# First batch of a fused attention and two-MLP kernel: another order of the weight conversions, other buffers, later scores

## Chip, cores, metric

One NeuronCore of a Trainium2 chip runs the whole program. The metric is device microseconds (us) of one execution. The kernel before takes a median of 846.8 us over three runs (846.05 to 849.2).

## What is computed

```python
scores = x @ state.T / sqrt(64)            # per batch (8) and head (8): 512 tokens, 32 state rows
xread  = softmax(scores) @ state           # 512 rows
sread  = softmax(scores.T) @ x             # 32 rows
x1 = concat(xread, sread)                  # 8 batches x 544 tokens x 512
h  = relu(x1 @ w_in)                       # 1024 features, padded at both ends
c  = conv_w[0]*h[t-1] + conv_w[1]*h[t] + conv_w[2]*h[t+1]
y  = (h * sigmoid(c)) @ w_out
k  = relu(mix_k(y) @ w_k);  r = sigmoid(mix_r(y) @ w_r);  out = r * (k*k @ w_v)
```

The weights come as 64-bit floats. The kernel reads their bits as pairs of 32-bit words and makes 32-bit values out of them on ScalarE (ACT) and VectorE (DVE).

## The kernel before

The work runs in slots. A slot is one token tile `t` (tiles 0 to 7 are the 512 tokens of a batch, tile 8 the state rows) and one block `f` of 128 features (8 of them). `g1_main` makes the product `hps` of the slot, `g1_a` drains it to `hb` (with relu) and starts the convolution, `g1_b` makes the gate `g`, `g1_c` splits it into a high and a low part `gs`, and `g1_sec` adds the slot's share of `y` to `acc` with three products for each of four output blocks: one with the high part (line 132), one each at lines 133 and 134 that need the low part as well or follow it. Batch 0 takes plain 32-bit products; for its first three blocks the convolution runs on TensorE (PE) too (`cps`, line 487), for all others on ACT (line 491) and DVE (line 493).

`x1 @ w_in` is never formed from `x1`: per batch, `m` (line 298) multiplies `state` with `w_in` into `p_m`, which is drained to `m_first` (batch 0) or `m_odd`/`me` (others), and `hps` is the softmax of the scores times that. The softmax of a batch (`max1`, `exp1`, `norm1`, `turn1`) is worked on DVE and ACT from the scores `p_s` (line 317) and ends in `a_first` (batch 0, line 374) or `aring` (others, lines 379 and 380). `exp2`, `turn2`, `sread` and `sturn` make the state rows.

At the start everything is missing. `w_in` and `w_out` come as four units each (two feature blocks, two transfers of 512 KB) and every unit is converted by `split` (lines 178 to 189): two passes on ACT (178 Abs, 180 Copy) and three on DVE (181, 182, 184), 1024 columns wide, and for `w_out` one more on ACT (188) and DVE (189). The first half of unit 0 of `w_in` is converted alone, 512 columns wide. PE is given idle products of the identity (`warm`, line 1079), 12 before the first scores, 14 behind them and 12 behind the first `m`.

A scheduler turns this into one instruction order per engine, by a priority for each piece. `at_half(k, fn, prio)` files a piece under half slot `k` (two per slot); `behind(i)` keeps what is written under it out of the order until `i` stands there; it adds no wait at run time. `attend(b, k, first)` files the attention of batch `b` from half slot `k` on, `M_PARTS` says at which half slots before the batch its products `m` come, and `weight_at` files load and conversion of a weight unit. Each engine then runs its list strictly in order. All transfers are issued by SP from one queue, with up to eight in flight: the ninth waits until the first has landed.

Of the kernel before, what the change touches and what calls it, by code (L numbers as in the profile page):

```python
# [25 lines left out]
ATTEND = 3  # L26
# [5 lines left out]
WARM = (12, 14, 12)  # L32
ATTEND_0, ATTEND_1 = 9, 3
# [3 lines left out]
def tile_kernel(  # L37
# [99 lines left out]
    class Weights:  # L137
# [24 lines left out]
        def split(self, w, first=0, whole=False):  # L162
# [21 lines left out]
            last = nc.vector.scalar_tensor_tensor(to, x, 3, v, op0=ALU.logical_shift_left, op1=ALU.bitwise_or)  # L184
# [25 lines left out]
    def weight(src, key, tag, pool, k, many, group):  # L210


        r = Weights([src[k + i] for i in range(many)], many, N, stg)

        def split(first=0, n=many):
            g = (key, "group", k // group)
            if k % group == 0 and first == 0:
                W[g] = pool.tile([P, 2, group, N], F32R, tag=f"{tag}{k // group}", name=f"{key}{k}")
            o = k % group + first
            for i in range(n):  # L220
                W[key, k + first + i] = W[g][:, :, o + i]
            return r.split(W[g][:, :, o:o + n], first)

        return r.load, split
# [57 lines left out]
    class Attention:  # L282
# [54 lines left out]
        def max1(self, g):  # L337
            q = self.q[:, g]
            nc.vector.transpose(q, self.v["s", g])
            q3 = q.rearrange("p (a n) -> p a n", n=NS)  # L340
            m1 = self.s1[:, g, 0]
            nc.vector.tensor_reduce(m1, q3, axis=AX.X, op=ALU.max)
            self.sub = nc.vector.tensor_tensor(
                q3, q3, m1.unsqueeze(2).to_broadcast([P, M1, NS]), op=ALU.subtract
            )
# [85 lines left out]
    anchors, y_stored, gated, last_ks = {}, {}, {}, {}  # L431
# [14 lines left out]
    def g1_main(t, f):  # L446
        p = ps_h.tile([P, 512], F32, tag="h", name="hps")
        if t < B:
            if t == 0:
                sl = slice(f * P, f * P + P)  # L450
                for g in range(G):
                    nc.tensor.matmul(p, m_first[:, g, sl], a_first[:, g], start=g == 0, stop=g == G - 1)
                st1[t, f] = {"p": p}
                return
# [42 lines left out]
    def g1_b(t, f):  # L497
# [5 lines left out]
        nc.vector.scalar_tensor_tensor(  # L503
# [557 lines left out]
    win = [weight_in(2 * i, 2, early[:, i] if i < 2 else None) for i in range(KF // 2)]  # L1061
# [32 lines left out]
    win[0][1](0, 1)  # L1094
# [3 lines left out]
    for g in range(G):  # L1098
        a.max1(g)
# [4 lines left out]
    for g in range(G):  # L1104
        a.turn1(g)
    with behind(a.sub):
        second = win[0][1](1, 1)
    second_m = a.m(1, 1)
    diagonals(0)
    nc.vector.tensor_scalar(om, muc, scalar1=-1.0, scalar2=1.0, op0=ALU.mult, op1=ALU.add)  # L1110
    with behind(second), behind(first_m):
        wout[0][1]()
    with behind(second):
        for g in range(G):
            a.max2(g)
    a.neg2()
    with behind(second_m):
        for g in range(G):
            a.exp2(g)

    def attend(b, k, first):
# [3 lines left out]
        if not first:  # L1125
# [9 lines left out]
            for i, d in enumerate(M_PARTS):  # L1135
                at_half(h + d, lambda i=i: a_.m(4 * i, 4), prio=500 * (h + d) - M_AHEAD)
# [23 lines left out]
    for f in range(1, KF):  # L1160
        if f % 2 == 0:
            weight_at(win[f // 2], 2 * f - 1, max(0, 2 * f - 5))
            at_half(2 * f - 1, lambda f=f: a.m(f, 2))
        if f < CONV_ON_PE:
            at_half(2 * f - 1, lambda f=f: diagonals(f))
    for f in range(2, KF, 2):
        weight_at(wout[f // 2], 2 * f + 5, 2 * f + 2)
    at_half(0, lambda: load_s(1, ap), lambda: load_t(1, ap), prio=-500)
    at_half(0, lambda: load_n(0, ap), prio=0)
    attend(0, ATTEND_0, True)  # L1170
    for b in range(1, B):
        attend(b, (b - 1) * H1 + (ATTEND if b > 1 else ATTEND_1), False)
    early_k = {j: weight_early(w_k, "k", 2 * j, h) for j, h in EARLY_AT.items()}
    for k, h in EARLY_V.items():
        load, split = weight(w_v, "v", "wa", wp, k, 2, 4)
# [130 lines left out]
```

## Time and profile before

| | |
|---|---|
| median of 3 runs | 846.8 us |
| the profiled execution itself | 847.35 us |
| its span, first to last instruction | 845.6 us |
| PE busy | 823.9 us, 97% |
| DVE busy | 694.9 us, 82% |
| ACT busy | 617.6 us, 73% |
| share of PE in the chain that ended last | 90% |
| mean granted TensorE clock | 0.992 of 2.4 GHz |

The table is an average over stages. The profile's 40 slices of the span show PE at 9 tenths or more everywhere but in the first, the third and the last slice (7, 8 and 7 tenths), and the granted clock below 9 tenths in the second slice alone. So the opening stretch, some 80 us long, has to be read by itself, wait by wait, in the order of time.

### The profile page before, as it was taken

Reading aid. Unit: us, or ns where it says so; the run is one execution under the profiler, and the core shown is the slowest. Engines: PE = TensorE matmul, PEld = TensorE weight load, DVE = VectorE, ACT = ScalarE, POOL = GpSimd, SP = SyncE. Lnnn points to the kernel's source line nnn. Section 1 sums busy time; section 2 is a strip of 40 time slices with the busy share of each in tenths; the row PEclk is TensorE's granted clock in tenths of the full one; section 3 lists DMA queues with packets and bytes.
Section 4 is the critical chain, followed back from the end, with each engine's and each line's share of the span. In section 5 each row is a group of like instructions: output and inputs, shape, how many; then the busy total and the mean of one; then the engine's idle time right before and its main releaser. Section 6 shows DMA issues by size and latency. Waiting matters only on the chain.

```text
span 845.6 us, 15213 instructions
## 1 busy us (share of the span) xinstructions
PE 823.9 (97%) x5766; PEld 701.8 (83%) x5766; DVE 694.9 (82%) x1110; ACT 617.6 (73%) x1163; POOL 10.3 (1%) x99
## 2 busy tenths in 40 slices
PE   7989999999999999999999999999999999999997
PEld 5345776676777666789998889999999999999997
DVE  5898787989988989887999789696978869596673
ACT  5688748678868688988976679767776876776652
POOL 0000000000000000000000000000000000000000
PEclk9899999999999999999999999999999999999999
DMA  9344312240505330905524855777878677775675
GB/s 340 131 147 156 107 50 107 78 179 7 199 30 179 129 112 1 349 26 193 199 84 175 282 190 174 226 239 247 255 228 262 217 239 260 227 251 180 218 253 194
DMA packets 68873, 150.50 MB, mean 178 GB/s; under 512 B 16064, under 2 KB 39616, under 8 KB 65984
## 3 DMA queue, kind: packets, MB, share of 16 engines
q1 hardware_dynamic: 68800, 149.53, 52.5%
q8 instruction: 45, 0.74, 0.4%
q14 instruction: 28, 0.23, 0.1%
HBM read 118.55 MB, written 30.97 MB: 177 GB/s over the span
## 4 chain that ended last, share of the span: by engine, by line
PE 90%; DVE 4%; ACT 3%; DMA 2%; issue 1%; SPq 0%; ACTq 0%; DVEq 0%
PE acc L132 14%; PE acc L133 13%; PE acc L134 13%; PE vps L133 6%; PE vps L132 6%; PE vps L134 6%; PE rps L133 3%; PE rps L134 3%; PE rps L132 3%; PE hps L132 3%; PE hps L134 3%; PE hps L133 3%; PE p_m L298 2%; PE hps L463 2%; PE p_s L317 2%; PE kps L132 1%
## 5 line engine op out<-in xcount | busy, mean ns | idle before, releaser
L493 DVE SCALAR_TENSOR_TENSOR cacc<-hb,vcol,cacc 128x512 f32<-128x512 f32 (+1 forms) x138 | 97.4, 719 | 19.7 <-ACT cacc L491 18.7
L133 PE MATMUL acc<-gs,out 128*128 128x512 f32 (+1 forms) x288 | 111.0, 386 | 0.2 <-DVE gs L512 0.2
L134 PE MATMUL acc<-gs,out 128*128 128x512 f32 (+1 forms) x288 | 109.7, 381 | 0.0
L132 PE MATMUL acc<-gs,out 128*128 128x512 f32 (+1 forms) x288 | 93.4, 396 | 1.2 <-ACT gs L511 0.6
L132 PEld LDWEIGHTS acc<-gs,out 128*128 128x128 f32 x288 | 53.0, 189 | 23.5 <-issue 4.2
L133 PEld LDWEIGHTS acc<-gs,out 128*128 128x128 f32 x288 | 54.2, 188 | 15.9 <-DVE aT L377 1.7
L134 PEld LDWEIGHTS acc<-gs,out 128*128 128x128 f32 x288 | 54.2, 188 | 12.6 <-issue 2.8
L132 PE MATMUL acc<-xo,k 128*128 128x256 f32 x224 | 63.3, 282 | 0.9 <-ACT stage L686 0.9
L134 PE MATMUL acc<-xo,k 128*128 128x256 f32 x224 | 63.1, 282 | 0.0
L133 PE MATMUL acc<-xo,k 128*128 128x256 f32 x224 | 62.9, 281 | 0.0
L511 ACT ACTIVATE gs<-g 128x512 fp32r<-128x512 f32 (+1 forms) x72 | 44.1, 612 | 17.9 <-PE acc L134 10.2
L512 DVE TENSOR_TENSOR gs<-g,gs 128x512 fp32r<-128x512 f32 (+1 forms) x72 | 47.0, 659 | 4.7 <-ACT gs L511 4.5
L503 DVE SCALAR_TENSOR_TENSOR g<-g,hb 128x512 f32<-128x512 f32 (+1 forms) x72 | 47.2, 657 | 3.4 <-ACT g L502 3.0
L475 ACT ACTIVATE hb<-hps 128x512 f32<-128x512 f32 x64 | 38.0, 599 | 16.4 <-PE hps L134 9.6
L132 PE MATMUL acc<-xo,kT 128*128 128x256 f32 x168 | 48.4, 288 | 1.0 <-ACT acc L855 1.0
L133 PE MATMUL acc<-xo,kT 128*128 128x256 f32 x168 | 48.4, 288 | 0.8 <-DVE xo L687 0.8
L491 ACT ACTIVATE cacc<-hb,vcol 128x512 f32<-128x512 f32 (+1 forms) x69 | 48.3, 701 | 0.4
L134 PE MATMUL acc<-xo,kT 128*128 128x256 f32 x168 | 48.3, 287 | 0.0
L133 PE MATMUL vps<-va,xa 128*128 128x256 f32 x168 | 47.6, 283 | 0.0
L132 PE MATMUL vps<-va,xa 128*128 128x256 f32 x168 | 47.6, 283 | 0.0
L134 PE MATMUL vps<-va,xa 128*128 128x256 f32 x168 | 47.5, 283 | 0.0
L502 ACT ACTIVATE g<-cacc 128x512 f32<-128x512 f32 (+1 forms) x69 | 42.2, 612 | 7.0 <-DVE cacc L493 6.2
(265 smaller groups left out, 2615.4 us busy)
## 6 DMA issues: line engine op xcount, KB each, us to landing
va<-vdT SPq DMA_DIRECT2D x38, 512.0 KB, 4.4
va<-vdB SPq DMA_DIRECT2D x28, 512.0 KB, 4.5
vb<-vdT SPq DMA_DIRECT2D x18, 512.0 KB, 4.2
xT<-x_t SPq DMA_DIRECT2D x32, 256.0 KB, 3.7
xn<-x_n SPq DMA_DIRECT2D x8, 1024.0 KB, 5.8
y<-yo SPq DMA_DIRECT2D x8, 1024.0 KB, 4.1
vb<-vdB SPq DMA_DIRECT2D x14, 512.0 KB, 4.8
va<-rdT SPq DMA_DIRECT2D x14, 512.0 KB, 4.6
```

The lines of the kernel that those rows point to most:

```text
L132: nc.tensor.matmul(ps, lh, rh, start=start and k == 0, stop=False, **how)
L133: nc.tensor.matmul(ps, lh, rl, start=False, stop=False, **how)
L134: nc.tensor.matmul(ps, ll, rh, start=False, stop=stop and k == last, **how)
L298: self.m_mm = nc.tensor.matmul(p[g][cols, :n * P].rearrange("p (f c) -> p f c", c=P), sT[self.b][r, c, h % 2], win_f[r, f:f + n, c * P:(c ...
L317: last = nc.tensor.matmul(self.v["s", g][cols, :], sT[self.b][r, h // 2, h % 2], xT[self.b][r, h // 2], start=True, stop=True,)
L475: nc.scalar.activation(hb[:, 1:1 + S], s["p"], AF.Relu)
L491: nc.scalar.activation(a[:, :n], hb[:, 0:n], AF.Copy, scale=w[0])
L493: nc.vector.scalar_tensor_tensor(a[:, :n], hb[:, k:k + n], w[k], a[:, :n], op0=ALU.mult, op1=ALU.add)
L502: nc.scalar.activation(g[:, :n], s["a"][:, :n], AF.Tanh, scale=0.5)
L503: nc.vector.scalar_tensor_tensor(g[:, :n], g[:, :n], 1.0, s["hb"][:, 1:1 + n], op0=ALU.add, op1=ALU.mult)
L511: act = nc.scalar.activation(gs[:, 0, :n], s["g"][:, :n], AF.Copy)
L512: dve = nc.vector.tensor_tensor(gs[:, 1, :n], s["g"][:, :n], gs[:, 0, :n].bitcast(F32), op=ALU.subtract)
```

## The change

It moves work within the opening and changes nothing that is computed.

- The idle products become 9 before the scores, 14 behind them, 12 behind the first `m`, and 6 new ones between the two halves of the first `hps` product.
- The first softmax is filed before the first conversion of `w_in`. The second half of unit 0 now stands behind unit 0 of `w_out`.
- Units 1 to 3 of `w_in` and `w_out` are filed by the tables `FIRST_IN` (half slot of the conversion, gate, half slot of `m`, half slot of the load) and `FIRST_OUT` (half slot of the conversion, gate, half slot of the load). The conversion stands behind the gate instruction `g` of the named slot.
- Units 2 and 3 of `w_in` are loaded into `early2`, a new tile in the place that `w_v` uses later (tag `wa1`), instead of the staging tile `raw`.
- The rest of batch 0's attention starts at half slot 5 instead of 9, batch 1's scores at 8 instead of 3, and batch 1's two `m` at half slots 14 and 15 instead of 10 and 12. Two loads move from half slot 0 to 1 and 4.

```diff
-WARM = (12, 14, 12)
-ATTEND_0, ATTEND_1 = 9, 3
+WARM = (9, 14, 12, 6)
+ATTEND_0, ATTEND_AT, M_AT = 5, {1: 8}, {1: (-2, -1)}
+
+FIRST_IN = {1: (2, -1, 3, 0), 2: (5, 0, 7, 0), 3: (8, 1, 9, 2)}
+FIRST_OUT = {1: (4, 0, 1), 2: (7, 1, 4), 3: (11, 2, 8)}
...
                 for g in range(G):
-                    nc.tensor.matmul(p, m_first[:, g, sl], a_first[:, g], start=g == 0, stop=g == G - 1)
+                    first = nc.tensor.matmul(p, m_first[:, g, sl], a_first[:, g], start=g == 0, stop=g == G - 1)
+                    if f == 0 and g == 0:
+                        with behind(first):
+                            warm(WARM[3])
...
-    win = [weight_in(2 * i, 2, early[:, i] if i < 2 else None) for i in range(KF // 2)]
+    early2 = wp.tile([P, 2, 2 * N * 2], U32, tag="wa1", name="early")
+    win = [weight_in(2 * i, 2, (early, early2)[i // 2][:, i % 2]) for i in range(KF // 2)]
...
-    win[0][1](0, 1)
+    for g in range(G):
+        a.max1(g)
+    with behind(a.turned):
+        win[0][1](0, 1)
     first_m = a.m(0, 1)
     with behind(a.m_mm):
         warm(WARM[2])
-    for g in range(G):
-        a.max1(g)
...
+    diagonals(0)
+    nc.vector.tensor_scalar(om, muc, scalar1=-1.0, scalar2=1.0, op0=ALU.mult, op1=ALU.add)
+    with behind(a.sub), behind(first_m):
+        wout[0][1]()
+    with behind(wout[0][2].merged):
+        for g in range(G):
+            a.max2(g)
+    a.neg2()
     with behind(a.sub):
         second = win[0][1](1, 1)
     second_m = a.m(1, 1)
...
+    for j in range(1, KF // 2):
+        w, g, m, load = FIRST_IN[j]
+        at_half(load, win[j][0])
+        at_half(w, behind_gate(win[j], g), prio=500 * w)
+        at_half(m, lambda j=j: a.m(2 * j, 2))
+        w, g, load = FIRST_OUT[j]
+        at_half(load, wout[j][0])
+        at_half(w, behind_gate(wout[j], g), prio=500 * w)
...
-    at_half(0, lambda: load_s(1, ap), lambda: load_t(1, ap), prio=-500)
-    at_half(0, lambda: load_n(0, ap), prio=0)
+    at_half(1, lambda: load_s(1, ap), lambda: load_t(1, ap), prio=-500)
+    at_half(4, lambda: load_n(0, ap), prio=0)
     attend(0, ATTEND_0, True)
     for b in range(1, B):
-        attend(b, (b - 1) * H1 + (ATTEND if b > 1 else ATTEND_1), False)
+        attend(b, ATTEND_AT.get(b, (b - 1) * H1 + ATTEND), False)
```

DVE, from the end of the small conversion of the convolution weights on: the kernel before (`early` and `mid` belong to the conversion of `w_in`, `q` to the softmax, `om` is the small mixing constant of a much later stage).

```order
L182 TENSOR_SCALAR mid<-mid 128x512
L339 STREAM_TRANSPOSE q<-p_s 128x512
L181 SCALAR_TENSOR_TENSOR early<-early 128x512
L1110 TENSOR_SCALAR om<-muc 128x8
L342 TENSOR_REDUCE s_154<-q 128x16
L339 STREAM_TRANSPOSE q<-p_s 128x512
L184 SCALAR_TENSOR_TENSOR w_in<-mid,early 128x512
```

The same place on DVE in the changed kernel.

```order
L344 STREAM_TRANSPOSE q<-p_s 128x512
L347 TENSOR_REDUCE s_152<-q 128x16
L1117 TENSOR_SCALAR om<-muc 128x8
L348 TENSOR_TENSOR q<-q,s_152 128x512
L344 STREAM_TRANSPOSE q<-p_s 128x512
L184 SCALAR_TENSOR_TENSOR early<-early 128x512
L185 TENSOR_SCALAR mid<-mid 128x512
L347 TENSOR_REDUCE s_152<-q 128x16
L372 TENSOR_REDUCE s_152<-q 128x16
L187 SCALAR_TENSOR_TENSOR w_in<-mid,early 128x512
```

The softmax's first transpose no longer stands behind a conversion pass; `om` now stands third, ahead of the second transpose, and the finished first half block of `w_in` comes three rows later.

ACT, around the first drain `hb` of batch 0: the kernel before.

```order
L178 ACTIVATE mid<-raw 128x1024
L180 ACTIVATE raw<-raw 128x1024
L355 ACTIVATE q<-q 128x512
L180 ACTIVATE early<-early 128x1024
L475 ACTIVATE hb<-hps 128x512
L476 ACTIVATE carry<-hb 128x2
L180 ACTIVATE raw<-raw 128x1024
L178 ACTIVATE mid<-early 128x1024
L502 ACTIVATE g<-cps 128x512
```

The same place on ACT in the changed kernel.

```order
L181 ACTIVATE mid<-raw 128x1024
L183 ACTIVATE raw<-raw 128x1024
L181 ACTIVATE mid<-early 128x512
L183 ACTIVATE early<-early 128x1024 x2
L183 ACTIVATE raw<-raw 128x1024
L483 ACTIVATE hb<-hps 128x512
L193 ACTIVATE out_231<-raw 128x1024
L181 ACTIVATE mid<-early 128x1024
L484 ACTIVATE carry<-hb 128x2
L181 ACTIVATE mid<-raw 128x1024
L183 ACTIVATE early<-early 128x1024
L510 ACTIVATE g<-cps 128x512
```

Ahead of `hb` there are now three full passes where there was one (the last of them, `raw`, is unit 1 of `w_out`), and four between `hb` and the gate's `g` where there were two.

PE, around batch 1's scores `p_s`: the kernel before (out_251 is unit 0 of `w_out`, out_415 unit 1).

```order
L317 MATMUL p_s<-xT,sT 32x512 x4
L452 MATMUL hps<-a_first,m_first 128x512
L317 MATMUL p_s<-xT,sT 32x512 x4
L452 MATMUL hps<-a_first,m_first 128x512
L132 MATMUL acc_376<-gs,out_251 128x512
```

The place of these scores on PE in the changed kernel (out_356 is unit 1 of `w_out`).

```order
L135 MATMUL acc_373<-gs,out_356 128x512
L423 MATMUL p_srT<-ident,sr 128x128
L322 MATMUL p_s<-xT,sT 32x512
L423 MATMUL p_srT<-ident,sr 128x128
L322 MATMUL p_s<-xT,sT 32x512 x3
L136 MATMUL acc_370<-gs,out_356 128x512
```

They stood before slot 1's share of `acc` (unit 0 of `w_out`) and now stand within slot 2's, behind the products of slots 3, 4 and 5 and the whole of batch 0's `sread`.

## Rows read from the trace of the kernel before

**Rows 1.** Stretch, length; PE, PEld, DVE, ACT, POOL busy (count); clock, DMA share, GB/s.
```profile
20.00:30.00 10.00, 8.67 (x28) 3.06 (x28) 10.00 (x15) 4.73 (x8) 0.10 (x1) 0.68 0.27 105
...
50.00:60.00 10.00, 7.89 (x37) 4.37 (x37) 9.50 (x20) 8.86 (x16) 0.48 (x1) 0.83 0.56 210
...
75.00:150.00 75.00, 75.00 (x489) 52.91 (x487) 57.57 (x95) 54.50 (x121) 1.72 (x17) 1.00 0.24 88
```

**Rows 2.** PE in order of time: start, us, what, [idle before <-its releaser].
```profile
1.41 5.11 PE L1079 MATMUL idle<-ident 128*128 128x128 f32 x24 [1.41 <-POOL hb L474]
6.45 1.54 PE L317 MATMUL p_s<-xT,sT 64*32 64x512 f32 x16
...
13.05 0.45 PE L298 MATMUL p_m<-w_in,sT 64*32 64x128 f32 x16 [1.74 <-DVE w_in L184]
13.43 2.94 PE L1079 MATMUL idle<-ident 128*128 128x128 f32 x24
17.63 1.10 PE L452 MATMUL hps<-a_first,m_first 128*128 128x512 f32 x2 [1.25 <-DVE a_first L374]
20.16 2.04 PE L452 MATMUL hps<-a_first,m_first 128*128 128x512 f32 x2 [1.44 <-DVE a_first L374]
22.90 4.59 PE L487 MATMUL cps<-hb,diag 128*128 128x512 f32 x6 [0.69 <-ACT hb L475]
...
28.35 1.98 PE L452 MATMUL hps<-a_first,m_first 128*128 128x512 f32 x4 [0.48 <-ACT m_first L305]
31.08 2.84 PE L487 MATMUL cps<-hb,diag 128*128 128x512 f32 x6 [0.75 <-ACT hb L475]
33.85 0.66 PE L298 MATMUL p_m<-w_in,sT 64*32 64x256 f32 x16
```

**Rows 3.** PE in order of time, the later part of the opening.
```profile
51.49 1.30 PE L298 MATMUL p_m<-w_in,sT 64*32 64x256 f32 x16 [2.76 <-ACT e L349]
53.38 1.77 PE L132 MATMUL acc<-gs,out 128*128 128x512 f32 x4 [0.58 <-ACT gs L511]
...
55.80 2.57 PE L452 MATMUL hps<-a_first,m_first 128*128 128x512 f32 x4
...
62.30 1.09 PE L298 MATMUL p_m<-w_in,sT 64*32 64x512 f32 x16
63.32 1.19 PE L132 MATMUL acc<-gs,out 128*128 128x512 f32 x4
...
68.33 1.23 PE L298 MATMUL p_m<-w_in,sT 64*32 64x256 f32 x16 [2.00 <-DVE m_odd L309]
...
78.20 1.06 PE L298 MATMUL p_m<-w_in,sT 64*32 64x512 f32 x8
...
79.28 0.48 PE L132 MATMUL hps<-aring,m_odd 128*128 128x512 f32 x1
```

**Rows 4.** DVE in order of time, same columns.
```profile
9.84 0.71 DVE L339 STREAM_TRANSPOSE q<-p_s 128x512 f32<-128x512 f32 x1
...
19.30 0.71 DVE L374 STREAM_TRANSPOSE a_first<-q 128x512 f32<-128x512 f32 x1
...
38.66 0.72 DVE L339 STREAM_TRANSPOSE q<-p_s 128x512 f32<-128x512 f32 x1 [0.72 <-PE p_s L317]
...
70.59 0.68 DVE L380 TENSOR_TENSOR aring<-aT,aring 128x512 fp32r<-128x512 f32 x1
```

**Rows 5.** Transfers issued from 4 to 13 us: count, KB each, us from issue to landing.
```profile
raw<-w_in SPq DMA_DIRECT2D x2, 512.0 KB, 10.8
...
muc<-mu SPq DMA_DIRECT2D x1, 4.0 KB, 5.7
```

**Rows 6.** SP's queue in order of time: start, us, what.
```profile
4.49 0.43 SPq L1069 DMA_DIRECT2D muc<-mu  x1
```

**Rows 7.** ACT in order of time: batch 0's first drain and gate.
```profile
22.24 0.60 ACT L475 ACTIVATE hb<-hps 128x512 f32<-128x512 f32 x1 [1.37 <-PE hps L452]
...
27.53 0.60 ACT L502 ACTIVATE g<-cps 128x512 f32<-128x512 f32 x1 [2.33 <-PE cps L487]
```

More of the change, by code (lines that the diff above doesn't have):

```diff
@@ L183, in split @@
             to = w.bitcast(U32) if whole else v
-            last = nc.vector.scalar_tensor_tensor(to, x, 3, v, op0=ALU.logical_shift_left, op1=ALU.bitwise_or)
+            last = self.merged = nc.vector.scalar_tensor_tensor(
+                to, x, 3, v, op0=ALU.logical_shift_left, op1=ALU.bitwise_or
+            )
             if whole:
@@ L222, in split @@
             return r.split(W[g][:, :, o:o + n], first)
-        return r.load, split
+        return r.load, split, r
     def weight_early(src, key, k, at):
@@ L338, in max1 @@
             q = self.q[:, g]
-            nc.vector.transpose(q, self.v["s", g])
+            self.turned = nc.vector.transpose(q, self.v["s", g])
             q3 = q.rearrange("p (a n) -> p a n", n=NS)
@@ L430, in tile_kernel @@
     st1 = {}
-    anchors, y_stored, gated, last_ks = {}, {}, {}, {}
+    anchors, gates, y_stored, gated, last_ks = {}, {}, {}, {}, {}
     def acc_tiles(key):
@@ L502, in g1_b @@
         nc.scalar.activation(g[:, :n], s["a"][:, :n], AF.Tanh, scale=0.5)
-        nc.vector.scalar_tensor_tensor(
+        gates[t * KF + f] = nc.vector.scalar_tensor_tensor(
             g[:, :n], g[:, :n], 1.0, s["hb"][:, 1:1 + n], op0=ALU.add, op1=ALU.mult
@@ L1108, in tile_kernel @@
     second_m = a.m(1, 1)
[L1109 to L1119, printed above, removed]
+    for g in range(G):
+        a.exp2(g)
     def attend(b, k, first):
@@ L1134, in attend @@
                 at_half(k + 3, lambda: load_s(b + 1, ap))
-            for i, d in enumerate(M_PARTS):
+            for i, d in enumerate(M_AT.get(b, M_PARTS)):
                 at_half(h + d, lambda i=i: a_.m(4 * i, 4), prio=500 * (h + d) - M_AHEAD)
@@ L1159, in tile_kernel, with behind_gate, split @@
     h2 = 2 * i0
[L1160 to L1167, printed above, removed]
-    at_half(0, lambda: load_s(1, ap), lambda: load_t(1, ap), prio=-500)
-    at_half(0, lambda: load_n(0, ap), prio=0)
+    def behind_gate(w, n):
+        def split():
+            with behind(gates[n] if n >= 0 else second):
+                w[1]()
+        return split
+    for j in range(1, KF // 2):
[6 more added lines that the diff above has]
+        at_half(w, behind_gate(wout[j], g), prio=500 * w)
+    for f in range(1, CONV_ON_PE):
+        at_half(2 * f - 1, lambda f=f: diagonals(f))
+    at_half(1, lambda: load_s(1, ap), lambda: load_t(1, ap), prio=-500)
+    at_half(4, lambda: load_n(0, ap), prio=0)
     attend(0, ATTEND_0, True)
     for b in range(1, B):
-        attend(b, (b - 1) * H1 + (ATTEND if b > 1 else ATTEND_1), False)
+        attend(b, ATTEND_AT.get(b, (b - 1) * H1 + ATTEND), False)
     early_k = {j: weight_early(w_k, "k", 2 * j, h) for j, h in EARLY_AT.items()}
     for k, h in EARLY_V.items():
-        load, split = weight(w_v, "v", "wa", wp, k, 2, 4)
+        load, split, _ = weight(w_v, "v", "wa", wp, k, 2, 4)
         at_half(h - 4, load)
```

## The prediction

> **What bounds the kernel now.** I read the busy shares first, then stretches of them, then PE by itself in the order of time, and only then the engines that PE waits for. Over the span PE is busy 97%, and from 75 to 150 us it works without a break at the full clock while DVE has 17.4 and ACT 20.5 of 75 us free [rows 1]. Nothing on DVE or ACT can be won there; whatever the change gains must be a wait or a low clock of PE in the opening. There the reader sees two kinds of loss. PE stands still: 1.74 us before the first `m`, 1.25 and 1.44 around the first `hps`, .69, .48 and .75 for the first drains [rows 2], later 2.76 (batch 1's `m`, behind the exponentials on ACT), .58 and 2.00 [rows 3]. And PE is slow: the mean granted clock is .68 from 20 to 30 us and .83 from 50 to 60 [rows 1]. Of its two levels, 1.2 and 2.4 GHz, the lower was granted for (1 − .68) × 2 × 10 = 6.4 us and (1 − .83) × 2 × 10 = 3.4 us. Each follows a stretch with two waits close together.
>
> **The change, part by part.** *The first softmax.* `p_s` is done at 6.45 + 1.54 = 7.99 us [rows 2], but the first transpose starts at 9.84 [rows 4], behind a conversion pass. The change frees it. The gain is mostly taken back by `om`, which now stands third on DVE: its `muc` is issued at 4.49 [rows 6] and lands 5.7 us later [rows 5], at 10.2, so the second transpose and the conversion passes behind it begin there, not at 8.6. With some .65 us for each 128x512 instruction (the rows of that size have .68 to .72 [rows 4] and overlap a little), the first half block of `w_in` is ready at 14.3 us instead of 13.0, and PE waits 3.1 us before the first `m` instead of 1.74. The second half of `a_first` comes at 19.1 instead of 19.30 + .71 = 20.0 [rows 4]; at full clock its half of `hps` (1.10 / 2 [rows 2]) ends at about 19.8, with pipeline and the first half 20.6 at the latest.
>
> *The first drain.* `hb` starts at 22.24 now [rows 7]. It will stand behind a pass on unit 1 of `w_out`. Transfers issued in this crowd of 512 KB took 10.8 us [rows 5]; counted in SP's order, this unit lands between 20.4 and 22.5. I take 21, and 1.1 us for the pass: `hb` at 22.1. So the early softmax is worth nothing here, what comes sooner on PE waits for ACT. Four passes follow, and the gate that came at 27.53 [rows 7] comes at 27.1; block 1's `hps` starts at 28.1 instead of 28.35 [rows 2]. **Gain .25.**
>
> *Idle products.* 38 become 41, each two entries of the trace, .213 us apiece in the first row (5.11 / 24, the low clock) and .12 behind the first `m` (2.94 / 24, full clock) [rows 2]. The three taken away stand ahead of the scores, which wait for their data. The six new ones, 6 × 2 × .12 = 1.4 us, fill the 1.44-us gap between the halves of `hps` [rows 2]. They are covered as long as `hb` waits for ACT until 22.1, 1.5 us after `hps` ends: cost nothing, and up to 1.4 if that cover goes.
>
> *Between 28 and 50 us.* The wait of .75 before block 1's `cps` [rows 2] is filled by block 0's first four `acc`. New waits: .23 (these `acc`, for the gate's `gs`) and .78 (the second half of an `hps`, for a drain of `m_first` on ACT), both from walking the new order with the durations of the rows. **Cost 1.0.**
>
> *Batch 1's scores and `m`.* PE waits at 51.49 and 53.38 because batch 1's exponentials and the gates meet 512 KB conversions on ACT, which is busy 8.86 of 10 us there, DVE 9.50 [rows 1]. With the scores at about 53 and 56 us and `m` behind them at half slots 14 and 15, the first `m` is reached at 65.55 and its exponentials are done at 65.65: the waits of 2.76, .58 and 2.00 go [rows 3], **5.34**, and .15 comes back. There is no margin at that point. Inside the `p_m` groups, 1.30 and 1.23 us against .66 for an undisturbed one of the same shape [rows 2, 3], another .64 + .57 = **1.2** of waiting goes. `m` is issued in four halves of 1.06 instead of partly whole at 1.09 [rows 3]: **cost 1.0**.
>
> *The low clock.* The second stretch follows the 2.76 and .58 us waits. Without them I expect it to go: `acc` x4 took 1.77 there and 1.19 elsewhere, `hps` x4 2.57 and 1.98 [rows 2, 3], 1.17 in these two groups, and over the 3.4 low us half of the time is lost, **1.7**. The first stretch I leave as it is, since ACT sets the end there; its rows say what it would give if it went and ACT were early: hps 2.04 − 1.10, cps 4.59 − 2.84 [rows 2], together 2.7. The page "TensorE: Matmul & The Clock Gate" of the Trainium skill, section "Terms", prices the throttled time at one minus the granted ratio, here half; for both stretches that would be 3.2 + 1.7, and the sum 3.2 us lower than mine. The rows agree on the second stretch; on the first, `hps` and `cps` account for 2.7.
>
> *Loads.* Two units of `w_in` go to `w_v`'s later place; `w_v` is loaded from half slot 42 on, and tile 1 begins at 16. They no longer wait for `raw` to come free, and the queue is not full after 30 us (DMA share .27 from 20 to 30 us [rows 1]). Counted at nothing; late landings of `w_out` unit 1 cost up to 1.5.
>
> *Sum:* idle .75 + 5.34, early .25, inside waits 1.2, clock 1.7, together 9.2; new waits 1.0 + .15, halves 1.0, together 2.2. Gain 7.0. The profiled execution took 847.35, so **840.3 us**. The median shown is .55 below it; by the same gain it would be 839.8. As a cross-check, tile 1's first `hps`, at 79.28 now [rows 3], falls to 74.35 in the walk, 4.9 earlier, and with eight `acc` products (at most 2 × 1.19) and half an `m` (1.06) more done by then [rows 3]: 7 to 8 us.
>
> **Rivals.** *DVE's debt.* At tile 1's start DVE will have nine 128x512 instructions fewer behind it (gates, `gs`, convolution sums, one `m_odd`), at .68 each [rows 4] 6.1 us. If PE meets it there, the gain is all but paid back: 846.4. For it: tile 1 leans on DVE from its first drain. Against it: DVE has 17.4 us free up to 150 [rows 1]. Chance .14.
>
> *The clock falls earlier.* If PE loses its clock in the 3.1 us before the first `m`, the 18 idle products behind it take .09 more per entry, 36 × .09 = 3.3, and `hps` .94 more: it ends at 24.8 instead of 20.6, and less the cover until 22.1 this costs 2.7: 843.0. For it: the low stretches follow waits. Against: after 1.74 alone and after 2.00 alone the clock stayed full [rows 2, 3]. The same page of the Trainium skill, section "What's actually happening", has the array go to the low rate after idling; a gap of 3.1 us does not stand in any row here. Chance .14.
>
> *Batch 1's softmax comes late (slower).* Its scores move some 17 us back, its use only as far as PE runs early. Before, from the first transpose to the finished `aring` it took 38.66 to 70.59 + .68, 32.6 us [rows 4]. I give it 15.7 (55.7 to 71.4), since the conversions that stood between will be done. If it takes 32.6 again, `aring` is ready at 88.3 and PE, which runs strictly in order, stands 14 us at tile 1's first `hps`: 854.3. It makes the kernel slower than before from an `aring` at 81.4, and by more than .5% from 85.1. For it: DVE at 9.5 of 10 and its debt. Against: only one unit of `w_out` is left to convert by then. Chance .08.
>
> **How the numbers follow.** About .5%, 4.2 us, is what a measurement of this kernel can tell from no change: below 842.6 is faster, above 851.0 slower. The forecast has .64, of it .57 faster (late transfers or lost cover take .07 into the same). The early clock gives .06 faster and .08 same, the debt .14 same, the late softmax .06 slower and .02 same. Sum: faster .63, same .31, slower .06. The range runs from 836.9, where the first low stretch goes as well (840.3 − 2.7 and .7 for the scatter of runs), to 846.5, the debt; it leaves out the late softmax and the tails, about .15.
>
> **What would show it.** Right: first transpose at 8.0, `om` waiting to 10.2; no PE wait of 2 us or more between 35 and 75; clock 1.00 from 50 to 60; tile 1's first `hps` near 74.4 with no wait before it; PE unbroken after 75. Wrong: a PE wait <- DVE `aring` (late softmax); waits <- DVE in tile 1 (debt); idle products at .21 after 14 us (early clock); `hb` after 23 us (transfers).

## The result and the profile after

The changed kernel takes a median of 837.35 us over four runs (836.11 to 837.71), beside 847.07 for the kernel before (846.05 to 849.2): a ratio of .9879, with a 95% interval from .9858 to .9901. That is 9.7 us less, where the prediction had 7.0 less and 840.3 us. The time lies at the low end of the range given (836.9), and as a ratio to the kernel before just below it (836.9 / 846.8 = .9883). The direction and most of the places were as forecast. Two steps were not, and one of them reverses what the change is to be credited with.

The page of the changed kernel, its span, PE's busy time and its two rows of 40 slices:

```profile
span 835.7 us, 15225 instructions
PE 820.9 (98%) x5772; PEld 703.1 (84%) x5772; DVE 694.4 (83%) x1110; ACT 619.1 (74%) x1163; POOL 10.5 (1%) x99
PE   7899999999999999999999999999999999999997
PEclk9999999999999999999999999999999999999999
```

PE's third slice, 8 tenths before, is at 9, its second, 9 before, at 8, and no slice's clock is below 9 tenths. The stretches that answer to [rows 1], with one around the only low clock of the opening:

```profile
16.50:19.80 3.30, 3.30 (x17) 3.30 (x17) 3.20 (x8) 3.30 (x4) 0.00 (x0) 0.50 1.03 413
...
50.00:60.00 10.00, 10.00 (x43) 5.05 (x42) 9.99 (x15) 7.22 (x17) 0.20 (x2) 1.00 0.65 229
...
75.00:150.00 75.00, 75.00 (x495) 54.65 (x480) 64.66 (x109) 58.70 (x125) 1.94 (x19) 1.00 0.26 88
```

From 50 to 60 us PE works without a break at the full clock, with DVE as busy as before. DVE's debt is visible from 75 to 150 us, 64.66 us of work where it had 57.57 [rows 1], and PE never waits for it there. PE in the order of time answers to [rows 2, 3]:

```profile
14.96 0.45 PE L303 MATMUL p_m<-w_in,sT 64*32 64x128 f32 x16 [3.29 <-DVE w_in L187]
15.34 4.51 PE L1088 MATMUL idle<-ident 128*128 128x128 f32 x24
19.64 1.13 PE L457 MATMUL hps<-a_first,m_first 128*128 128x512 f32 x2
20.61 1.50 PE L1088 MATMUL idle<-ident 128*128 128x128 f32 x12
21.95 1.02 PE L457 MATMUL hps<-a_first,m_first 128*128 128x512 f32 x2
23.66 2.84 PE L495 MATMUL cps<-hb,diag 128*128 128x512 f32 x6 [0.69 <-ACT hb L483]
...
28.60 1.98 PE L457 MATMUL hps<-a_first,m_first 128*128 128x512 f32 x4 [1.72 <-ACT m_first L310]
30.63 1.20 PE L135 MATMUL acc<-gs,out 128*128 128x512 f32 x4
31.66 2.74 PE L495 MATMUL cps<-hb,diag 128*128 128x512 f32 x6
...
38.79 0.66 PE L396 MATMUL p_a<-ident,e 128*128 128x128 f32 x4 [0.44 <-ACT m_first L310]
...
68.76 1.06 PE L303 MATMUL p_m<-w_in,sT 64*32 64x512 f32 x8 [0.48 <-ACT m_first L310]
...
75.59 0.50 PE L135 MATMUL hps<-aring,m_odd 128*128 128x512 f32 x1
```

The waits of 1.25, 1.44, .75, 2.76, .58 and 2.00 are gone; 3.29 and 1.72 stand where 1.74 and .48 stood, and .44 and .48 are new. The low clock fell on idle products and on the start of `hps` (24 entries in 4.51 us, 2.94 before), and the first `cps` ran at the full clock, 2.84 instead of 4.59. DVE and ACT beside it:

```profile
10.81 0.17 DVE L1117 TENSOR_SCALAR om<-muc 128x8 f32<-128x8 f32 x1 [2.20 <-DMA muc<-mu]
...
18.92 0.71 DVE L379 STREAM_TRANSPOSE a_first<-q 128x512 f32<-128x512 f32 x1
```

```profile
21.69 1.19 ACT L183 ACTIVATE raw<-raw 128x1024 uint32<-128x1024 uint32 x1 [0.46 <-DMA raw<-w_out]
23.01 0.60 ACT L483 ACTIVATE hb<-hps 128x512 f32<-128x512 f32 x1
...
27.75 0.63 ACT L510 ACTIVATE g<-cps 128x512 f32<-128x512 f32 x1
28.23 0.49 ACT L310 ACTIVATE m_first<-p_m 128x128 f32<-128x128 f32 x2
```

**A ledger in three parts.** To tell the opening from the rest, each profiled execution is cut at two products of PE: tile 1's first `hps` (79.28 us before, 75.59 after) and the first product of the second stage, `acc<-xo,k`. What stands ahead of the first cut beyond the kernel before is taken off: with the scores at half slot 8 these are eight `acc` products (.23 each from one start to the next, 1.82) and half an `m` (.99 from its start to that of the next product), 2.81 together. So the opening took 75.59 − 2.81 = 72.8 against 79.3: **6.5 us won there**, the forecast's 7.0. The second cut, in both kernels, first the one before, with PE's waits of .2 us and more on the way to it:

```profile
292.22 0.50 PE L133 MATMUL acc<-gs,out 128*128 128x512 f32 x1 [0.24 <-DVE gs L512]
296.87 0.73 PE L132 MATMUL hps<-aring,me 128*128 128x512 f32 x2 [0.24 <-ACT aring L379]
...
349.17 0.50 PE L132 MATMUL acc<-gs,out 128*128 128x512 f32 x1 [0.58 <-ACT yo L530]
...
483.81 0.36 PE L132 MATMUL acc<-xo,k 128*128 128x256 f32 x1 [0.90 <-ACT stage L686]
```

```profile
474.13 0.36 PE L135 MATMUL acc<-xo,k 128*128 128x256 f32 x1 [0.42 <-DVE r L673]
```

The middle took 483.81 − 79.28 = 404.5 before and 474.13 − 75.59 + 2.81 = 401.4 after: **3.2 us won behind tile 1**, where the prediction had counted nothing. Of these 1.5 are in the waits shown (.24 + .24 + .58 + .90 − .42). The other 1.7 lie in no single row. Products with 32 columns (`p_m`, `p_s`, `p_sr`) and full ones change places 78 times in the middle before and 70 after, and a change costs time: the first full product behind `p_m` or `p_s` starts .52 us after the last one ahead of it, an `acc` behind an `acc` .23. Worked out from the starts of these rows, and without the change that the half `m` brings, this is some 1.2 us, an estimate; the rest is open. The end, 361.8 and 361.6, is the same.

All runs in this ledger, from their profiled executions, with the ratio of their times to the kernel before (its median beside them was 847.1 to 847.8). One of e2's four executions, 909.14 us at a mean granted clock of .843, is left out of its row and its time:

| run | edit | ratio (95%) | opening | middle | end |
|---|---|---|---|---|---|
| before | | 1 | 79.3 | 404.5 | 361.8 |
| changed | | .9879 (.9858, .9901) | 72.8 | 401.4 | 361.6 |
| e1 | before + later scores | .9980 (.9967, .9992) | 81.4 | 401.4 | 362.0 |
| e9 | before + new home | .9974 (.9958, .9990) | 80.4 | 401.6 | 362.7 |
| e10 | before + both | .9935 (.9919, .9952) | 75.2 | 401.5 | 362.2 |
| e7 | changed, old home | 1.0005 (.9992, 1.0017) | 83.5 | 401.4 | 361.2 |
| e2, e12 | changed, scores at 3 | 1.0068 (1.0049, 1.0088) | 78.7 | 411.3 | 363.0 |
| e14 | changed, scores at 6 | .9980 (.9969, .9990) | 80.6 | 400.7 | 362.4 |
| e5 | changed, no gates | .9936 (.9914, .9958) | 77.2 | 401.3 | 362.1 |
| e6 | changed, `w_out` late | .9896 (.9872, .9920) | 74.8 | 401.3 | 361.8 |
| e3 | changed, old softmax | .9901 (.9882, .9920) | 75.5 | 401.3 | 362.1 |
| e4 | changed, no gap products | .9883 (.9863, .9903) | 72.7 | 401.4 | 361.5 |
| e8 | changed, `om` late | .9887 (.9859, .9915) | 73.9 | 401.4 | 362.6 |
| e11 | e8, unit 1 of `w_out` late | .9876 (.9859, .9893) | 73.8 | 401.3 | 361.5 |
| e13 | e11, other idle products | .9874 (.9848, .9900) | 71.8 | 402.1 | 361.1 |

For e12 batch 0's state rows, 1.7 us of PE, come behind the first cut and are counted into its opening. One profiled execution can stand a few us beside its kernel's median (e10's is the fastest of its four runs, 840.74, its median 842.26). Up to the first `cps`, e1, e9 and e10 have the same waits of 1.25, 1.44 and .69 us (to .01), and `cps` takes 4.50, 4.38 and 2.84: the low clock alone moves an opening by 1.7 us. Differences of the openings under 2 us are not read by themselves.

The middle is steadier, and the traces say why. In the eleven kernels with the scores at half slot 8 (the changed one, e1, e3 to e8, e10, e11, e13), PE, DVE and ACT run the same instructions in the same order from tile 1's first `hps` to the end, and the middle is 401.3 to 402.1, with openings from 71.8 to 83.5. The kernel before, e9, e12 and e14 each have an order of their own.

### The profile page after: what moved, and what is told of

It is laid out like the page before. It is cut to its first block, busy times and chain, and to the rows that moved or that the text cites. A ratio compares the mean times of both kernels' runs of the same rounds, so it can differ in the third digit from the quotient of the medians.

```text
span 835.7 us, 15225 instructions
## 1 busy us (share of the span) xinstructions
PE 820.9 (98%) x5772; PEld 703.1 (84%) x5772; DVE 694.4 (83%) x1110; ACT 619.1 (74%) x1163; POOL 10.5 (1%) x99
## 4 chain that ended last, share of the span: by engine, by line
PE 95%; DMA 2%; DVE 1%; ACT 1%; SPq 0%; issue 0%; DVEq 0%; ACTq 0%
PE acc L135 14%; PE acc L136 14%; PE acc L137 14%; PE vps L136 6%; PE vps L135 6%; PE vps L137 6%; PE rps L137 3%; PE rps L136 3%; PE rps L135 3%; PE hps L135 3%; PE hps L136 3%; PE hps L137 3%; PE p_m L303 3%; PE p_s L322 2%; PE hps L471 2%; PE hps L457 2%
## 5 line engine op out<-in xcount | busy, mean ns | idle before, releaser
L137 PEld LDWEIGHTS acc<-gs,out 128*128 128x128 f32 x288 | 54.1, 188 | 15.9 <-issue 6.1
```

The costliest lines, as they stand in the source:

```text
L137: nc.tensor.matmul(ps, ll, rh, start=False, stop=stop and k == last, **how)
```

## The experiments

**The scores alone, and the change without them (e1, e2, e12).**

```diff
 (to the kernel before)
-ATTEND_0, ATTEND_1 = 9, 3
+ATTEND_0, ATTEND_1, M_AT = 5, 8, {1: (-2, -1)}
```

> The kernel before with one part of the change alone: the rest of batch 0's attention at half slot 5, batch 1's scores at half slot 8 and its two m at half slots 14 and 15; conversions, loads, buffers and idle products as before. Theory 1 (the later scores carry the gain, in the opening and by the order of the work behind it): 837.5 to 840 us, no PE wait of 2 us or more between 45 and 75 us, no low clock there, and about 3 us won behind tile 1's first hps as in the changed kernel. Rival 2 (the gates and loads of the conversions carry it): 844 us or more, with a PE wait behind ACT or DVE of 2 us or more still there.

845.59 us against 847.61. The time and the waits are Rival 2's; of theory 1 only the 3 us behind tile 1 came. PE's waits did not go, they moved from `m` to `acc`, behind the gates of the late slots. PE of e1:

```profile
60.44 1.06 PE L317 MATMUL p_s<-xT,sT 64*32 64x512 f32 x8 [1.10 <-ACT aux L426]
65.36 1.19 PE L132 MATMUL acc<-gs,out 128*128 128x512 f32 x4 [1.81 <-ACT gs L511]
69.48 0.79 PE L133 MATMUL acc<-gs,out 128*128 128x512 f32 x1 [2.94 <-DVE gs L512]
```

The opening became 2 us longer (81.4). The whole gain, and more, is in the middle (401.4).

```diff
 (to the changed kernel)
-ATTEND_0, ATTEND_AT, M_AT = 5, {1: 8}, {1: (-2, -1)}
+ATTEND_0, ATTEND_AT, M_AT = 9, {1: 3}, {}
```

> The changed kernel with that part alone undone: rest of batch 0's attention at half slot 9, batch 1's scores at 3, its m at 10 and 12. Theory 1: 844 to 847.5 us, the waits before batch 1's m are back and the 3 us behind tile 1 are lost. Rival 2: 841 us or less.

> The run with the scores at half slot 3 once more, for its profile at the full clock. It was 854 us, slower than the kernel before. Theory 10 (batch 1's softmax on DVE and ACT falls between conversions that now come earlier): acc waits for gs and m waits for e between 45 and 80 us, 3 us or more in all, with a low clock behind them, and tile 1 begins 5 us or more later than before after the correction for work done by then. Rival 14 (the time is lost behind tile 1): tile 1 begins as before, and the 7 us are lost in waits between 80 and 480 us.

854.13 us (e2) and 854.79 (e12): slower than the kernel before, which neither theory for e2 expected. Both halves of the expectation for e12 hold in part. The opening has the waits (PE of e12), and behind tile 1 there are others:

```profile
51.70 1.19 PE L135 MATMUL acc<-gs,out 128*128 128x512 f32 x4 [3.31 <-ACT gs L519]
54.15 1.08 PE L303 MATMUL p_m<-w_in,sT 64*32 64x256 f32 x8 [1.26 <-ACT e L354]
...
165.15 1.85 PE L135 MATMUL acc<-gs,out 128*128 128x512 f32 x4 [2.23 <-ACT gs L519]
...
312.11 1.20 PE L135 MATMUL acc<-gs,out 128*128 128x512 f32 x4 [0.76 <-ACT gs L519]
315.65 0.50 PE L135 MATMUL hps<-aring,me 128*128 128x512 f32 x1 [0.94 <-ACT hb L483]
```

The opening is about that of the kernel before (78.7), the loss is the middle's: 411.3. PE's waits of .2 us and more there come to 6.3 us, where the kernel before has 2.0, and behind the one of 2.23 the clock was .50 for 3.4 us. So Rival 14 names the place where the 7 us went, and most of them are in rows.

**The new home (e7, e9, e10).** The prediction had counted it at nothing.

```diff
 (e7, to the changed kernel; e9 and e10 make the same edit the other way round in the kernel before)
-    early2 = wp.tile([P, 2, 2 * N * 2], U32, tag="wa1", name="early")
-    win = [weight_in(2 * i, 2, (early, early2)[i // 2][:, i % 2]) for i in range(KF // 2)]
+    win = [weight_in(2 * i, 2, early[:, i] if i < 2 else None) for i in range(KF // 2)]
```

> The changed kernel with units 2 and 3 of w_in loaded into the staging tile raw again instead of w_v's later home. The prediction counted the other home at nothing: 837 to 838.2 us. Rival 8 (the transfers wait for raw to come free, and later transfers behind them in the queue): PE waits for w_in, m_first or w_out of 1.5 us or more between 30 and 60 us, 839 to 842 us.

847.91 us: the whole gain is gone. SP's queue shows why, first in the changed kernel, then in e7 (x4 stands for two units of two transfers each; the second unit of the first row starts at 40.8 us):

```profile
27.51 14.13 SPq L163 DMA_DIRECT2D raw<-w_out  x4
46.27 0.80 SPq L163 DMA_DIRECT2D raw<-w_v  x2
```

```profile
27.39 0.81 SPq L163 DMA_DIRECT2D raw<-w_out  x2
39.14 0.80 SPq L163 DMA_DIRECT2D raw<-w_in  x2
40.24 0.80 SPq L163 DMA_DIRECT2D raw<-w_out  x2
55.55 0.80 SPq L163 DMA_DIRECT2D raw<-w_out  x2
```

What SP waited for longest in e7 from 20 to 62 us (us in all, times, the longest one):

```profile
SPq L163 <- DVE w_in L187: 18.8, 2, 10.9
```

The staging tile `raw` has two buffers, and a load into one waits for the last pass on the unit that lay there. When units of `w_in` pass through it too, the last unit of `w_out` is issued at 55.6 us instead of 40.8. Its seven passes on ACT and DVE then fall between 60.5 and 72.4 us, where the gates of the late slots and batch 1's softmax have to run, and PE waits as in e1. PE of e7, and the stretch behind the first of these waits:

```profile
62.39 0.50 PE L136 MATMUL acc<-gs,out 128*128 128x512 f32 x1 [1.91 <-DVE gs L520]
...
67.19 2.07 PE L135 MATMUL acc<-gs,out 128*128 128x512 f32 x4 [1.66 <-ACT gs L519]
...
70.73 0.79 PE L136 MATMUL acc<-gs,out 128*128 128x512 f32 x1 [1.47 <-DVE gs L520]
```

```profile
63.20:76.80 13.60, 10.47 (x24) 7.27 (x23) 13.39 (x26) 5.40 (x10) 0.20 (x2) 0.50 0.41 148
```

The waits are 5 us. Of the 13.6 us at the lower level of the clock, 1.2 GHz, PE worked 10.47, at the upper level half of that: some 5 us more, an estimate, of the 10.7 by which the opening grew. The rival had the queue right. It had PE's waits wrong: between 30 and 60 us none is above .32, they are for `gs` behind 60; and it was too small in price, since it had no low clock in it.

> The kernel before with the new home for units 2 and 3 of w_in alone (loaded into w_v's later place, all else as before). Theory 10 (home and later scores only work together: the home frees raw, so that w_out is converted before batch 1's softmax, but the scores at half slot 3 bring that softmax into the conversions): 844 to 850 us. Rival 11 (the home alone carries the gain): 837 to 841 us.

> The kernel before with two parts of the change: the new home and the later scores of batch 1 (with the rest of batch 0's attention earlier). Theory 10: these two carry nearly all: no wait of acc for gs of over 1 us between 55 and 75 us, no low clock there, 837 to 841 us. Rival 12 (the gates and earlier half slots are needed too): 842 to 846 us.

845.32 and 842.26 us. In the opening the two parts do not add up, they need each other: the scores alone cost 2.1 us, the home alone wins nothing, both together win 4.1 (81.4, 80.4 and 75.2 against 79.3). So far theory 10. But 2.7 of the 4.1 are the first low clock, which fell on `hps` and `cps` in the kernel before [rows 2] and not in e10's execution, and that the two carry nearly all is not borne out: e10's median lies in Rival 12's range, and a wait for `gs` that theory 10 had excluded is left. PE of e10:

```profile
65.27 0.50 PE L133 MATMUL acc<-gs,out 128*128 128x512 f32 x1 [1.49 <-DVE gs L512]
```

By the ratios the two win 5.5 of some 10.2 us; gates, half slots, softmax and idle products together win the other 4.7.

**Another place for the scores (e14).**

```diff
-ATTEND_0, ATTEND_AT, M_AT = 5, {1: 8}, {1: (-2, -1)}
+ATTEND_0, ATTEND_AT, M_AT = 5, {1: 6}, {1: (-2, -1)}
```

> The changed kernel with batch 1's scores at half slot 6 instead of 8; conversions, loads and m as in the change. Theory 17 (the time between tile 1's first hps and the second stage is set by the order that the scheduler happens to make behind the edit: 404.5 us before, 401.4 in every run with the scores at 8, some 411 with them at 3): that stretch comes out at another value than 401.4, by over 1 us, and PE's waits in it name the same places as in no other run. Rival 18 (it is set by whether the scores come behind the conversions): 401.0 to 401.8 again. For the opening both expect 72.8 to 78 us after the correction for work done by then, for the whole 837 to 845 us.

845.72 us. The opening, 80.6, lies outside what both expected: PE waits 2.19 and 2.41 us for `gs`, as in e12, and the clock is .50 from 53.3 to 59.9. The middle, 400.7, is .7 from 401.4, between the two expectations, in another order; within one order it ranges from 401.3 to 402.1, so this run does not settle them.

**Gates, `w_out`'s half slots, the first softmax (e5, e6, e3).**

```diff
 (e5)
-            with behind(gates[n] if n >= 0 else second):
-                w[1]()
+            w[1]()
```

> The changed kernel with the conversions filed at the same half slots but not behind the gate instructions. Theory 4 (the gates keep conversion passes from standing in front of the slots' own drains and gates on ACT and DVE): the passes come earlier, PE waits for hb, g or gs between 20 and 60 us, 2 us or more, 839.5 to 843 us. Rival 5 (the half slots alone do it): 837 to 838 us.

842.47 us; opening 77.2. Theory 4's time, and not the waits that it named: the one wait of over 2 us from 20 to 60 us is 2.52 for `m_first` on ACT, 1.72 in the changed kernel, with low clocks around it; since the low clock fell elsewhere than in the changed kernel too (15.1 to 21.9 us and 32.1 to 35.5), how much is the gates' own queueing and how much the clock stays open.

```diff
 (e6)
-        w, g, load = FIRST_OUT[j]
-        at_half(load, wout[j][0])
-        at_half(w, behind_gate(wout[j], g), prio=500 * w)
+        weight_at(wout[j], 4 * j + 5, 4 * j + 2)
```

> The changed kernel with units 1 to 3 of w_out loaded and converted at the half slots of before (6, 10 and 14) and without gates. Theory 6 (with the scores moved to half slot 8, the late conversions of w_out meet batch 1's softmax on ACT and DVE, as in the run that moved the scores alone): waits of acc for gs of 1.8 and 2.9 us and a low clock between 60 and 75 us, 842 to 846 us. Rival 7 (those waits come from the conversions of w_in): 837 to 839.5 us.

839.31 us, and no wait for `gs` of over .2 us from 55 to 75 us: theory 6 falls. With `raw` free, the old half slots of `w_out` are early enough. The table `FIRST_OUT` is worth some 2 us at these medians, and the two intervals overlap; the home is what matters.

```diff
 (e3: WARM, and the order of the first softmax and the first conversions)
-WARM = (9, 14, 12, 6)
+WARM = (12, 14, 12, 0)
...
-    for g in range(G):
-        a.max1(g)
-    with behind(a.turned):
-        win[0][1](0, 1)
+    win[0][1](0, 1)
     first_m = a.m(0, 1)
...
+    for g in range(G):
+        a.max1(g)
...
-    with behind(a.sub), behind(first_m):
+    with behind(second), behind(first_m):
         wout[0][1]()
```

> The changed kernel with the first softmax, the first conversions and the idle products (12, 14, 12, none between the halves) as before. Theory 1 (ACT, not the softmax, sets the end of the first 30 us; the early softmax is worth at most .5 us): 837 to 838.5 us. Rival 3 (the gain over the forecast came from the low clock that now falls on idle products instead of hps and cps): 839.5 to 841 us, with hps and cps at the low clock again from 20 to 26 us.

839.67 us, in Rival 3's range but not by its mechanism: the first `hps` and `cps` ran at the full clock (1.10, 1.10 and 2.84 us), and the 2.7 us of opening went into a wait of 2.67 us for `w_in` at 30.2 us, one of .90 for `gs`, one of 1.41 for `hb`, and a low clock from 32.4 to 35.8. The early softmax, the order of the conversions and the idle products that go with it are worth some 2.3 us by the medians; the intervals overlap, and the edit does not tell the three apart. The first `cps` itself starts at 22.98 us, .7 before the changed kernel's.

**The first 30 us (e4, e8, e11, e13).**

```diff
 (e4)
-WARM = (9, 14, 12, 6)
+WARM = (9, 14, 12, 0)
```

> The changed kernel without the six idle products between the halves of the first hps. Theory 1: the second half of hps ends 1.2 us sooner, but hb waits on ACT behind the pass on w_out until about 22.9 anyway, so 837.0 to 837.6 us, no difference. Rival 3 (these products keep the clock up): the low clock falls on hps or cps and costs 1 to 2.7 us, 838.4 to 840 us.

837.63 us: no difference, as expected, and not for the reason given. Without the six products the scheduler put `hb` ahead of the pass on `w_out` on ACT, and it starts 1.3 us sooner. ACT, then PE of e4:

```profile
21.70 0.60 ACT L483 ACTIVATE hb<-hps 128x512 f32<-128x512 f32 x1 [0.43 <-PE hps L457]
22.20 1.18 ACT L183 ACTIVATE raw<-raw 128x1024 uint32<-128x1024 uint32 x1
```

```profile
30.46 1.20 PE L135 MATMUL acc<-gs,out 128*128 128x512 f32 x4 [0.73 <-ACT gs L519]
```

By the first `acc` all but .17 us of it is gone again (30.63 in the changed kernel). So this run does not test whether `hb` waits for that pass; e8 does.

```diff
 (e8)
-    nc.vector.tensor_scalar(om, muc, scalar1=-1.0, scalar2=1.0, op0=ALU.mult, op1=ALU.add)
+    with behind(a.sub):
+        nc.vector.tensor_scalar(om, muc, scalar1=-1.0, scalar2=1.0, op0=ALU.mult, op1=ALU.add)
```

> The changed kernel with om behind the first softmax on DVE, so that no instruction waits for muc until 10.8 us. Theory 1 (hb waits on ACT for the pass on unit 1 of w_out, which lands at 21.7 us): the first m comes 2 us sooner, hb does not, 837 to 837.8 us; up to 1.7 more if the low clock then falls on hps and cps. Rival 9 (the 2.2 us of DVE are on the path): 835 to 836 us.

838.41 us. Theory 1, with its low clock; the first `m` came 1.0 us sooner (13.94), not 2. PE was done with `hps` at 20.3 us, 2.7 sooner than in the changed kernel, and then stood for 4.06, since ACT held `hb` behind a pass whose data had not landed. PE, then ACT of e8:

```profile
24.38 4.54 PE L495 MATMUL cps<-hb,diag 128*128 128x512 f32 x6 [4.06 <-ACT hb L483]
```

```profile
22.74 1.10 ACT L183 ACTIVATE raw<-raw 128x1024 uint32<-128x1024 uint32 x1 [1.30 <-DMA raw<-w_out]
23.75 0.58 ACT L483 ACTIVATE hb<-hps 128x512 f32<-128x512 f32 x1
```

This pass belongs to unit 1 of `w_out`, which is filed behind the gate of slot 0. The gate is an instruction of DVE. This unit's DVE passes stand behind it; the ACT pass stands ahead of `hb` in the order all the same, as the rows of ACT's order ahead of the prediction show.

```diff
 (e11, to e8)
+    hbs = {}
...
-            nc.scalar.activation(hb[:, 1:1 + S], s["p"], AF.Relu)
+            hbs[t * KF + f] = nc.scalar.activation(hb[:, 1:1 + S], s["p"], AF.Relu)
...
             with behind(gates[n] if n >= 0 else second):
-                w[1]()
+                if late is None:
+                    w[1]()
+                else:
+                    with behind(hbs[late]):
+                        w[1]()
...
-        at_half(w, behind_gate(wout[j], g), prio=500 * w)
+        at_half(w, behind_gate(wout[j], g, j if j == 1 else None), prio=500 * w)
```

> The changed kernel with om behind the first softmax and both of unit 1 of w_out's passes on ACT behind the drain hb of block 1 instead of ahead of the drain of block 0. The gate of a unit is an instruction of DVE and holds DVE's passes alone, so one ACT pass of this unit stood ahead of hb and waited for its transfer to 21.7 us. Theory 1 (that pass and ACT's in-order queue set the first 30 us): hb at about 21.5 instead of 23.0, block 1's hps at about 26.9 instead of 28.6, PE's order unchanged, 834.5 to 836.5 us. Rival 13 (what PE gains there it gives back at a drain of m_first or at acc of block 2, for which this unit comes late): 837 to 839 us.

837.55 us, Rival 13's time, but not by what it named: block 1's `hps` started at 26.90, as theory 1 had it, and the clock took it back. PE of e11, and the stretch:

```profile
26.90 3.78 PE L458 MATMUL hps<-a_first,m_first 128*128 128x512 f32 x4 [2.34 <-ACT m_first L310]
29.69 2.69 PE L135 MATMUL acc<-gs,out 128*128 128x512 f32 x4
```

```profile
26.10:32.80 6.70, 5.90 (x9) 3.17 (x10) 4.85 (x10) 4.84 (x12) 0.10 (x1) 0.50 0.69 268
```

```diff
 (e13, to e11)
-WARM = (9, 14, 12, 6)
+WARM = (9, 14, 19, 0)
...
     second_m = a.m(1, 1)
-    for g in range(G):
-        a.exp2(g)
+    with behind(a.m_mm):
+        warm(10)
+    with behind(second_m):
+        for g in range(G):
+            a.exp2(g)
```

> The run e11 (om and unit 1 of w_out's ACT passes later) with the idle products placed otherwise: 19 instead of 12 behind the first m and none between the halves of the first hps, and 10 new ones behind block 1's m, where PE waited 2.34 us for m_first; batch 0's exponentials behind that m_first on ACT. In e11 block 1's hps did start at 26.9 us as expected, but the low clock from 26.1 to 32.9 us took it back (hps x4 3.78 instead of 1.98, acc x4 2.69 instead of 1.20). Theory 15 (that low clock followed the waits of .69, .56 and 2.34 us; with these filled it does not come there): full clock from 20 to 35 us and 833.5 to 836 us. Rival 16 (the clock falls anyway, or the idle products come in the way of hps): 837 us or more.

836.84 us. The clock is full from 0 to 480 us (1.00 in that stretch), as theory 15 says, and `hps` and `acc` have their 1.98 and 1.20 us back; the mean granted clock of its four runs is .998 to 1.000, of the changed kernel's .996 to .999. The time is .8 above its range: the opening gained 1.0 over the changed kernel, and the middle, in the same order, lost .7 again. Against the changed kernel the intervals lie on each other (.9874 and .9879), so this is no better kernel that could be shown, only another of the same time.

## Why the prediction was right or wrong

**What bounds the kernel:** right. The gain of the opening came from PE's waits and from the second low clock, and tile 1 and what follows stayed PE's.

**The sum for the opening:** right in size (7.0 forecast, 6.5 measured), wrong in what it was put down to, so that the size is luck in part. The waits of 2.76, .58 and 2.00 were said to go because the scores stand later. The products that stood 2.76 and 2.00 us were not batch 1's: their rows have 64x256 elements, two feature blocks, as batch 0's `m` has; batch 1's have 64x512 [rows 3]. They waited for a place to write: `p_m`, `p_s`, `p_a` and `p_sr` share the two buffers of the pool `ps_a`, and batch 1's scores held both until its exponentials `e` had read them, later its first `m` until that was drained to `m_odd`. With later scores batch 0's `m` of blocks 4 and 5 no longer waits. But e1 shows that this alone only moves the waits, to 1.10, 1.81 and 2.94. They go when the softmax comes later and the conversions are finished before it, and these finish early because `w_in` leaves `raw` to `w_out`: the last pass on `w_out` ends at 54.8 us in the changed kernel, at 72.4 in e7, and at 70.7 in the kernel before.

**"Loads ... counted at nothing":** this step failed. The argument was that the queue is not full and that `w_v` comes much later. Both are true, and the limit was a third thing, the two buffers of `raw`: a load waits for the passes on the unit that lies there. Without the new home the opening is 10.7 us longer (e7).

**Nothing behind tile 1:** this step failed too, by 3.2 us, and it makes the difference between forecast and result. The sum took the work behind tile 1 as unchanged, because the diff is in the opening. But the scheduler made another order down to the second stage. That it is the order and not an earlier or emptier start is shown by e1 and e7: tile 1 starts 8.6 and 10.7 us later there than in the changed kernel, by the ledger, the three engines run the same order from there on, and the middle is the same 401.4. That it is not the later scores as such is shown by e9, where they stand at half slot 3 and the middle is 401.6. The ledger's fifteen kernels have only five orders behind tile 1: three take 400.7 to 402.1, those of the kernel before (404.5) and of e12 (411.3) are the poor ones. Why the scheduler made those two is not settled.

**The first drain:** the mechanism was right (`hb` behind the pass on `w_out`, the early products covered) and the times 1 us early: the transfer landed at 21.7 and `hb` started at 23.01, not 22.1. In this kernel `hps` ended at 22.97 and that pass at 22.88, so that both set it. The first half block of `w_in` was late as well, 14.90 us for 14.3, since `muc` let `om` start at 10.81 and not at 10.2. Block 1's `hps` began at 28.60, .25 behind the kernel before, where .25 sooner was forecast: all of the 6.5 us lies behind it. "The early softmax is worth nothing here" holds for this drain: in e3, without it, the first `cps` starts .7 us sooner, and what e3 lost it lost at 30.2 us, by the order of the conversions.

**New waits:** .23 and .78 were forecast between 28 and 50 us, .44 was measured; `m_first` at 28.6 took 1.72, where the walk had PE only .25 sooner than before. The point without a margin, the `m` behind batch 1's exponentials, is batch 0's last one (64x256); it was reached at 67.62 and not at 65.55, .4 us behind the end of `e` and with no wait of its own. Batch 1's first `m` follows at 68.76 behind the .48 for `m_first`. It came as two halves and one whole, as in the kernel before, and not as four halves, so the 1.0 put down for halves was not paid.

**The low clock and its rival:** the second stretch went, as forecast. For the first, the rival's event took place, and not at its price. PE stood 3.29 us before the first `m`, and from 16.5 to 19.8 us the granted clock was .50. The Trainium skill's page "TensorE: Matmul & The Clock Gate", section "What's actually happening", has the array fall to the low rate after idling, and this trace agrees. But the low clock now lay on idle products, whose length is covered by ACT, and left `cps` alone: the 4.59 us of [rows 2] became 2.84. The price given, 2.7 us on top, had the low clock on all 36 idle entries behind the first `m` and on `hps`; it lasted over the first 24 (1.57 us longer) and left the twelve entries between the halves at 1.50 us and `hps` at 1.13. And the price forgot what the same low clock had cost elsewhere before.

**The other rivals:** DVE's debt exists and was not paid on the path. The softmax of batch 1 took from 56.56 to 72.4 us (the last `aring` starts with its pair at 71.13, 1.28 us long), 15.9 where 15.7 was forecast and the slower rival had 32.6; PE reached it at 75.59.

## What to carry to other kernels

Before a load is counted at nothing, look not only at the queue and at who needs its old place later, but at how many buffers its staging tile has and who else passes through it. Two edits that each look like the cause may each be worth little alone (.9980 and .9974 here) and need each other: try each alone and both. When a product waits for an engine that it takes no operand from, ask who still holds the buffer that it is to write. And where a scheduler orders the program, an edit in the opening is an edit of everything behind it; cut the time at a landmark and compare the parts, before a difference is put down to the place of the edit.

## What the runs showed of the hardware

What the lower clock level costs can be read from the same rows at both levels: 1.57 us on 24 idle entries in the changed kernel (4.51 for 2.94), 1.70 on `cps` in e8 (4.54 for 2.84), 1.80 and 1.49 on `hps` and `acc` in e11. It followed single waits of 3.29 us (changed kernel) and 4.06 us (e8), and in e11 three waits of .69, .56 and 2.34 us within 6.9 us, while it did not follow single ones of 1.74 and 2.00 [rows 2, 3] or 1.74 in e13. The waits alone do not tell it: behind the same 1.25, 1.44 and .69 us of e1, e9 and e10 the clock was .50 in e1 and e9 from 22.6 to 25.5 us, and 1.00 there in e10. In e7 it lasted 13.6 us although PE was busy for 10.47 of these. Idle products in front of real ones took it upon themselves in the changed kernel, where another engine set the end anyway, at next to no cost: `hb` started .13 us behind ACT's pass.
